# The first loads of v moved ahead of two pairs' q and k, and the first two pairs' splits shared out anew: a fused attention and MoE kernel

## The chip, the core and the metric

The kernel runs on one core of one Trainium2 chip. The metric is the device time of one execution in microseconds (us): the median of three runs. A core has TensorE (PE in the rows; PEld is its weight load), VectorE (DVE), ScalarE (ACT), GpSimd (POOL) and SyncE (SP). SP computes nothing here; it issues almost every transfer, one after the other, in the order in which the program was written. Each engine works off its own queue in order and waits on semaphores for the others.

## The reference

Causal attention over 2 batches x 12 heads, 448 positions, 64 channels a head, then two dense layers that the code calls MoE:

```python
scores = (q @ k.T) / 8;  scores = where(above the diagonal, -1e9, scores)
attn   = exp(scores - max);  attn = attn / (sum + 1e-9);  a = attn @ v       # per head
x = a laid out as 896 x 768
h = max(x@w1, x@w2, x@w3) @ w_out                # w1..w3: 768 x 768, w_out: 768 x 768
g = s * relu(h @ w_in)**2 + b                    # w_in: 768 x 2048
out = g @ w_out2                                 # 896 x 768
```

All inputs are float32. The kernel keeps float32 accuracy by writing each operand as a rounded part and a remainder, hi + lo, and by forming hi·hi + lo·hi + hi·lo on TensorE.

## The kernel before

The 24 heads are worked off as 12 pairs; one pair fills 128 partitions (two heads x 64 channels). `attention` runs 14 steps, `step(s)` for s = 0 to 13. In step s, three pairs are in flight: `new` = s (scores, minima, exponentials), `old` = s - 1 (transposes of the exponentials, row sums) and `out` = s - 2 (the product with v, `pv`). The MoE layers follow, with TensorE fed by decoded weight tiles.

A pair's data comes in as the tile `R`, 128 x (q, k) x 448, by `load(p)` (L268): 448 KB, one transfer, except pair 0, which comes in two. The pool behind `R` has four buffers, so pairs 0 to 3 are loaded ahead of step 0 and `load(4)` stands at the end of step 0. From `R` the tile `HL` is made: q hi, q lo, k hi, k lo. For pair 0 that is `split_now` (L330 to L340), called for columns 0 to 255 and for 256 to 447; for pair 1 it is `split_hi_early` on GpSimd and `split_lo_early` on VectorE. For pairs from 2 on, `scaled` (L296) multiplies q in `R` by -1/8 on GpSimd, `split_hi` (L309) rounds q and k on VectorE, and `split_lo` (L92) takes the remainders on GpSimd. `both_tails` copies the last 64 columns into the tile `bd` (L296). The order on GpSimd is the program's: `bd` of pair 0; hi of pair 1; `bd` of pair 1; `scaled(2)`, `scaled(3)`; a memset in `v` (L596); lo of pair 2; `bd` of pair 2; a memset in `v` (L606); lo of pair 3; `bd` of pair 3; `scaled(4)`.

The scores are written to PSUM (tiles A, B and C). `minima` (L396) takes row minima on VectorE, `exps` (L408) writes `p` on ScalarE, `transposes` (L435) turns `p` on TensorE, `pt_copy` (L441) brings it back. `pv` (L451, L455, L460) multiplies by v into the tile `o`, of which there is one buffer.

The row sums take a round trip through DRAM. `spread` copies them to `rows` (L487, VectorE) and SP writes them out as `rcd` (L488, L489). `broadcast` reads them back, spread over 64 partitions, as `rb` (L497, two transfers). `pv_out` (L506, VectorE) multiplies `o` by `rb` into `xf`. The next `pv` can't write `o` before that. `rcd` and `rb` of pair s - 1 are issued in step s; `xf` of pair s - 3 is computed in step s.

v comes in as four groups of pairs (`V_GROUPS`: first pair, number of pairs), each as seven pieces, and for a group of more than one pair as seven pieces for each head. Their elements are 256 bytes long. `V_LOADS` says how many pieces each step issues, before and behind its `rb`; 42 pieces in all. `FETCH` names the steps that fetch a weight tile `wraw` (L129, 768 KB).

The transfers share eight completion semaphores (DMAHW0 to DMAHW7 in the order below), given out in turn: a transfer waits on SP until the one eight before it has landed, and everything behind it on SP waits with it.

Of the kernel before, what the change touches and what calls it, by code (L numbers as in the profile page):

```python
# [14 lines left out]
ALU = mybir.AluOpType  # L15
# [9 lines left out]
NQ = 3  # L25
# [10 lines left out]
    7: ("low2",), 8: ("clamp2",), 9: ("shift2",), 10: ("hi1", "sign2"), 11: ("high3",),  # L36
    12: ("hi2", "low3"),
}
V_GROUPS = ((0, 1), (1, 1), (2, 4), (6, 6))
V_LOADS = ((7, 7), (2, 5), (3, 4), (3, 0), (3, 0), (3, 0), (3, 0), (2, 0))  # L40
FILL = {12: (3, 5), 13: (0, 4)}
WARM = 10
BUSY = (7,)
# [7 lines left out]
def kernel(  # L51
# [14 lines left out]
    nc = tc.nc  # L66
    n_pairs = qk.shape[0]
    S = qk.shape[3]
# [10 lines left out]
    scale = 1.0 / float(D) ** 0.5  # L79
# [11 lines left out]
    def sub_lo(eng, lo, full, hi):  # L91
        eng.tensor_tensor(out=lo, in0=full, in1=hi.bitcast(F32), op=ALU.subtract)  # L92
# [139 lines left out]
    def attention():  # L232
        with ExitStack() as c2:
# [10 lines left out]
            vs = [  # L244
                fixed.tile([128, n, 2, NQ + 1, D], F32, name=f"v{a}") for a, n in V_GROUPS
            ]
# [18 lines left out]
            def load(p, cuts=((0, S),)):  # L265
                pair[p]["R"] = R = ld.tile([128, 2, S], F32, tag="R", name="R")
                for a, b in cuts:
                    nc.sync.dma_start(out=R[:, :, a:b], in_=qk[p, :, :, a:b])  # L268
# [4 lines left out]
            def v_loads(g):  # L273
                (first, n), V = V_GROUPS[g], vs[g]
                for a, b in pieces:
# [7 lines left out]

            v_list = [e for g in range(len(V_GROUPS)) for e in v_loads(g)]

            def load_v(n):
                for _ in range(min(n, len(v_list))):
                    to, of = v_list.pop(0)
                    nc.sync.dma_start(out=to, in_=of)  # L289

            def v_of(p):
                g = max(g for g, (a, _) in enumerate(V_GROUPS) if a <= p)
                return vs[g][:, p - V_GROUPS[g][0]]

# [27 lines left out]
            def split_lo_early(p):  # L322
                HL, R = pair[p]["HL"], pair[p]["R"]
                nc.vector.scalar_tensor_tensor(
                    out=HL[:, 1], in0=R[:, 0], scalar=-scale, in1=HL[:, 0].bitcast(F32),
                    op0=ALU.mult, op1=ALU.subtract,
                )
                sub_lo(nc.vector, HL[:, 3], R[:, 1], HL[:, 2])

            def split_now(p, a, b, eng):  # L330
                HL, R = pair[p]["HL"], pair[p]["R"]
                q, k = (R[:, n, a:b] for n in range(2))
                qh, ql, kh, kl = (HL[:, n, a:b] for n in range(4))
                nc.vector.tensor_scalar(out=qh, in0=q, scalar1=-scale, scalar2=None, op0=ALU.mult)
                nc.scalar.copy(out=kh, in_=k)
                nc.vector.scalar_tensor_tensor(
                    out=ql, in0=q, scalar=-scale, in1=qh.bitcast(F32),
                    op0=ALU.mult, op1=ALU.subtract,
                )
                sub_lo(eng, kl, k, kh)  # L340

            def both_tails(p):
                HL = pair[p]["HL"].bitcast(F32)
# [27 lines left out]
            def at(p, i):  # L371
                a, b = ((2 * TQ, 3 * TQ), (0, 2 * TQ), (0, 3 * TQ))[i]
                return pair[p]["A" if i == 2 else "B"][:, :, a:b]
# [19 lines left out]
            def minima(p, i):  # L393
                e = pair[p]
                src, cols = (at(p, i), slice(2 * i, 2 * i + 2)) if i < NQ else (e["C"][:, 0:S], slice(2 * NQ, 2 * NQ + 1))
                nc.vector.tensor_reduce(  # L396
                    out=e["mx"][:, cols], in_=src, axis=mybir.AxisListType.X, op=ALU.min
                )
# [115 lines left out]

            CUT = 2 * TQ
            load(0, ((0, CUT), (CUT, S)))
            for p in range(1, 4):
                load(p)
            keep_busy(WARM)
            make_identity(nc, ident)  # L520
# [3 lines left out]
                out=tri.rearrange("p (a n) -> p a n", a=2), in_=tri.rearrange("p (a n) -> p a n", a=2), pattern=[[0, 2], [-1, TQ]], base=0, channel_multiplier=1,  # L524
# [8 lines left out]
            for P in ps:  # L533
                nc.gpsimd.memset(P[:, L0 + S:PW], 0.0)
            new_hl(0)
            split_now(0, 0, CUT, nc.vector)
            split_now(0, CUT, S, nc.gpsimd)
            both_tails(0)
            split_hi_early(1)
            first = early_products()  # L540
# [10 lines left out]
            def step(s):  # L551
                new, old, out, nxt = (
                    p if 0 <= p < n_pairs else None for p in (s, s - 1, s - 2, s + 2)
                )
                loads = V_LOADS[s] if s < len(V_LOADS) else (0, 0)
                if new is not None:
# [29 lines left out]
                    mask_c(new)  # L586
                    scores_c(new)
                if new == 0:
                    for i in (0, 1, 2, NQ):
                        minima(new, i)  # L590
                    split_lo_early(1)
                    both_tails(1)
                    for n in (2, 3):
                        scaled(n)
                    for V in vs[:2]:
                        nc.gpsimd.memset(V[D:128, :, :, NQ, :], 0.0)  # L596
                elif new is not None:
                    minima(new, 2)
# [43 lines left out]
                if old is not None:  # L642
# [2 lines left out]
                        spread(old)  # L645
                    transposes(old, 2)
                    transposes(old, 3)
                if new == 0:
                    load_v(loads[0])
                if s + 4 < n_pairs:  # L650
                    load(s + 4)
                if old is not None:
# [174 lines left out]
    with tc.manual_schedule():  # L827
        attention()
        moe()
# [50 lines left out]
```

## Time and profile before

| | us |
|---|---|
| median of 3 runs | 502.41 (501.32 to 503.15) |
| profiled execution, its own time | 502.06 |
| its span, first instruction to last | 500.3 |
| PE busy / DVE / ACT / POOL | 493.3 / 340.5 / 282.9 / 71.4 |
| PE's granted clock, mean | 0.999 of full speed |

The span is what the trace covers; the execution's own time is 1.76 us more, around it. Times in rows count from the span's start. A row of the timeline gives start, duration, engine, line, operation, tiles written and read, shapes, how many instructions are merged (x2), and in brackets how long the engine had been idle just before and what ended that. SPq is SP issuing a transfer: its duration is the issue, not the transfer. A busy PE is a modelled figure, so small gaps in it are rough.

### The profile page before, as it was taken

The page shows a single profiled execution, that of the slowest core. Times are in us where ns is not written, and L with a number is a line of the kernel's source. Part 1 is how long each engine was busy: PE and PEld are TensorE (multiplying, and loading weights), DVE is VectorE, ACT ScalarE, POOL GpSimd, SP SyncE. Part 2 cuts the span into 40 slices and gives each one's busy share as a digit, 9 for nine tenths or more (in the row PEclk, how much of TensorE's full clock was granted, in tenths as well). Part 3 has the DMA queues.
Part 4 walks back from the last instruction along what each step waited for, and adds up shares of the span by engine and source line. Part 5 has one row for each costly group of instructions (what it writes and reads, how often), then busy time and mean ns, then how long its engine had stood idle before and what let it go on. Part 6 is the DMA issues. An engine that isn't in the chain of part 4 may idle for free.

```text
span 500.3 us, 7557 instructions
## 1 busy us (share of the span) xinstructions
PE 493.3 (99%) x2909; PEld 452.7 (90%) x2909; DVE 340.5 (68%) x512; ACT 282.9 (57%) x527; POOL 71.4 (14%) x103
## 2 busy tenths in 40 slices
PE   8999999999999999999999999999999999999997
PEld 4877888899999999999999999999999999999996
DVE  5778896665857667587677888888888644484401
ACT  5988977444445254444546878888786432253101
POOL 6988992300000000000000000000000000000000
PEclk9999999999999999999999999999999999999999
DMA  5777534223324231333223323332333323261003
GB/s 170 225 215 226 151 102 117 103 91 127 126 75 148 94 126 64 126 128 126 101 89 126 127 73 118 126 104 85 127 126 109 119 89 128 88 220 56 1 0 111
DMA packets 26212, 58.34 MB, mean 117 GB/s; under 512 B 13548, under 2 KB 17600, under 8 KB 26176
## 3 DMA queue, kind: packets, MB, share of 16 engines
q1 hardware_dynamic: 26032, 57.76, 35.2%
q8 instruction: 23, 0.38, 0.3%
q14 instruction: 13, 0.11, 0.1%
q10 hardware_dynamic: 144, 0.10, 0.1%
HBM read 55.05 MB, written 2.80 MB: 116 GB/s over the span
## 4 chain that ended last, share of the span: by engine, by line
PE 91%; DMA 2%; DVE 2%; SPq 2%; ACT 1%; POOL 1%; issue 0%; DVEq 0%; ACTq 0%
PE m L698 58%; PE m L807 23%; PE t L435 3%; PE o L451 2%; ACT p L408 1%; PE o L455 1%; SPq L289 1%; PE A L380 1%; PE C L388 1%; PE B L380 1%; DMA rcd<-rows 1%; DMA rb<-rcd 1%; DMA R<-in_qk_dram 1%; POOL HL L92 0%; PE o L460 0%
## 5 line engine op out<-in xcount | busy, mean ns | idle before, releaser
L698 PE MATMUL m<-x,whi 128*128 128x448 f32 x816 | 232.0, 366 | 0.0
L698 PEld LDWEIGHTS m<-x,whi 128*128 128x128 f32 x816 | 153.1, 188 | 12.3 <-ACT p L408 0.2
L698 PE MATMUL m<-x,wlo 128*128 128x448 f32 x408 | 149.0, 365 | 0.0
L807 PE MATMUL m<-whi,g 128*128 128x384 f32 x448 | 114.0, 334 | 0.0
L184 ACT CAST whi<-wa 128x768 fp32r<-128x768 f32 x56 | 46.7, 833 | 67.0 <-PE m L807 43.8
L698 PEld LDWEIGHTS m<-x,wlo 128*128 128x128 f32 x408 | 76.6, 188 | 6.0
L807 PEld LDWEIGHTS m<-whi,g 128*128 128x128 f32 x448 | 81.0, 188 | 0.0
L144 ACT ACTIVATE wa<-wraw 128x768 f32<-128x768 f32 x56 | 50.6, 904 | 52.3 <-DVE wlo L92 52.3
L92 DVE TENSOR_TENSOR wlo<-wa,whi 128x768 fp32r<-128x768 f32 x56 | 53.3, 953 | 38.4 <-ACT whi L184 38.4
L807 PE MATMUL m<-wlo,g 128*128 128x384 f32 x224 | 74.8, 334 | 0.0
L179 DVE CUSTOM_DVE_ANT_0 wa<-wa,wr 128x1536 uint16<-128x1536 uint16 x56 | 53.6, 957 | 1.9
L172 DVE SCALAR_TENSOR_TENSOR wa<-wraw,wa 128x768 int32<-128x768 int32 x56 | 53.7, 959 | 0.0
L147 ACT ACTIVATE wr<-wraw 128x768 int32<-128x768 uint32 x56 | 50.6, 904 | 0.0
L807 PEld LDWEIGHTS m<-wlo,g 128*128 128x128 f32 x224 | 42.0, 188 | 0.0
L705 DVE TENSOR_TENSOR t<-t,m 128x448 f32<-128x448 f32 x24 | 14.9, 621 | 38.7 <-PE m L698 38.7
L698 PE MATMUL m<-h,whi 128*128 128x448 f32 x144 | 40.9, 365 | 0.0
L166 DVE TENSOR_SCALAR wa<-wa 128x768 int32<-128x768 int32 x56 | 32.2, 575 | 1.8
L92 POOL TENSOR_TENSOR HL<-R,HL 128x448 fp32r<-128x448 f32 (+1 forms) x21 | 29.9, 1443 | 3.2 <-DVE HL L309 2.1
L792 ACT ACTIVATE r<-m 128x448 f32<-128x448 f32 x32 | 17.4, 544 | 22.2 <-PE m L698 22.2
L698 PEld LDWEIGHTS m<-h,whi 128*128 128x128 f32 x144 | 27.1, 188 | 2.1
L158 DVE TENSOR_SCALAR wa<-wa 128x768 f32<-128x768 f32 x52 | 28.7, 552 | 0.0
L781 DVE SCALAR_TENSOR_TENSOR r<-m,r 128x448 f32<-128x448 f32 x32 | 20.0, 625 | 12.3 <-ACT r L792 12.3
(85 smaller groups left out, 551.2 us busy)
## 6 DMA issues: line engine op xcount, KB each, us to landing
wraw<-in_w_dram SPq DMA_DIRECT2D x56, 768.0 KB
R<-in_qk_dram SPq DMA_DIRECT2D x11, 448.0 KB
rb<-rcd SPq DMA_DIRECT2D x24, 112.0 KB
out_dram<-o SPq DMA_DIRECT2D x13, 192.0 KB
v<-in_v_dram SPq DMA_DIRECT2D x4, 96.0 KB
v<-in_v_dram SPq DMA_DIRECT2D x2, 168.0 KB
v<-in_v_dram SPq DMA_DIRECT2D x6, 48.0 KB
v<-in_v_dram SPq DMA_DIRECT2D x2, 144.0 KB
```

Source lines behind the costliest of these rows:

```text
L92: eng.tensor_tensor(out=lo, in0=full, in1=hi.bitcast(F32), op=ALU.subtract)
L144: nc.scalar.activation(out=e["f"], in_=e["high"].bitcast(F32), func=ACTF.Abs)
L147: nc.scalar.activation(out=e["r"], in_=e["low"].bitcast(U32), func=ACTF.Copy, scale=2.0 ** -29)
L158: nc.vector.tensor_scalar(out=e["f"], in0=e["f"], scalar1=UNDER, scalar2=OVER, op0=ALU.max, op1=ALU.min)
L166: nc.vector.tensor_scalar(out=a, in0=a, scalar1=3, scalar2=0x3FFFFFF8, op0=ALU.logical_shift_left, op1=ALU.bitwise_and,)
L172: nc.vector.scalar_tensor_tensor(out=e["a"], in0=e["high"], scalar=-0x40000000, in1=e["a"], op0=ALU.bitwise_and, op1=ALU.bitwise_or,)
L179: nc.vector.tensor_tensor(out=e["a"], in0=e["a"], in1=e["r"], op=ALU.add)
L184: nc.scalar.copy(out=e["hi"], in_=e["f"])
L698: nc.tensor.matmul(p, wt[w][:, ws], cols(act[i], a, b), start=(i == 0 and n == 0), stop=(i == len(act) - 1 and n == 2),)
L781: nc.vector.scalar_tensor_tensor(out=r, in0=p, scalar=0.0, in1=r, op0=ALU.max, op1=ALU.mult)
L792: after(0, lambda: nc.scalar.activation(out=r, in_=p, func=ACTF.Relu))
L807: nc.tensor.matmul(acc[t][:, 0:EH], gt[f][:, a, ts], w[:, ws], start=(f == 0 and n == 0), stop=(f == KG - 1 and n == 2),)
```

## The change

Three things change. On SP, the first seven pieces of v go ahead of the loads of pairs 2 and 3; the groups of v become pairs 0, 1, 2 to 4 and 5 to 11 (they were 0, 1, 2 to 5 and 6 to 11); and the pieces are given to other steps: 11 behind the weight tile in step 0, 4 and 6 in step 1, none in step 2, then 4, 4, 3 and 3 in steps 3 to 6, all ahead of `rb`. In `split_now`, columns 256 to 447 of q hi go from VectorE to ScalarE, and k lo of the same columns from GpSimd to VectorE. On VectorE, the minimum of pair 0's tile C goes from ahead of pair 1's q lo to behind it.

```diff
-V_GROUPS = ((0, 1), (1, 1), (2, 4), (6, 6))
-V_LOADS = ((7, 7), (2, 5), (3, 4), (3, 0), (3, 0), (3, 0), (3, 0), (2, 0))
+V_GROUPS = ((0, 1), (1, 1), (2, 3), (5, 7))
+V_LOADS = ((0, 11), (4, 6), (0, 0), (4, 0), (4, 0), (3, 0), (3, 0))
...
                     op0=ALU.mult, op1=ALU.subtract,
                 )
+                minima(0, NQ)
                 sub_lo(nc.vector, HL[:, 3], R[:, 1], HL[:, 2])
 
-            def split_now(p, a, b, eng):
+            def split_now(p, a, b):
...
-                nc.vector.tensor_scalar(out=qh, in0=q, scalar1=-scale, scalar2=None, op0=ALU.mult)
                 nc.scalar.copy(out=kh, in_=k)
+                if a:
+                    nc.scalar.mul(out=qh, in_=q, mul=-scale)
+                    sub_lo(nc.vector, kl, k, kh)
+                else:
+                    nc.vector.tensor_scalar(
+                        out=qh, in0=q, scalar1=-scale, scalar2=None, op0=ALU.mult
+                    )
                 nc.vector.scalar_tensor_tensor(
                     out=ql, in0=q, scalar=-scale, in1=qh.bitcast(F32),
                     op0=ALU.mult, op1=ALU.subtract,
                 )
-                sub_lo(eng, kl, k, kh)
+                if not a:
+                    sub_lo(nc.vector, kl, k, kh)
...
             load(0, ((0, CUT), (CUT, S)))
-            for p in range(1, 4):
+            load(1)
+            load_v(7)
+            for p in range(2, 4):
                 load(p)
...
-                    for i in (0, 1, 2, NQ):
+                    for i in range(NQ):
                         minima(new, i)
...
-                if new == 0:
-                    load_v(loads[0])
                 if s + 4 < n_pairs:
                     load(s + 4)
```

SP at the start of the program, before; R_135 is pair 0, R_138, R_140 and R_142 are pairs 1 to 3, R_251 is pair 4:

```order
L268 DMA R_138<-in_qk_dram 128x896
L268 DMA R_140<-in_qk_dram 128x896
L268 DMA R_142<-in_qk_dram 128x896
L289 DMA v0_112<-in_v_dram 112x2x64
L289 DMA v0_112<-in_v_dram 16x2x64
L289 DMA v0_112<-in_v_dram 96x2x64
L289 DMA v0_112<-in_v_dram 32x2x64 [waits DMAHW0_49]
L289 DMA v0_112<-in_v_dram 80x2x64 [waits DMAHW1_49]
L289 DMA v0_112<-in_v_dram 48x2x64 [waits DMAHW2_49]
L289 DMA v0_112<-in_v_dram 64x2x64 [waits DMAHW3_49]
L268 DMA R_251<-in_qk_dram 128x896 [waits DMAHW4_49,DVE_49,Pool_49]
L129 DMA wraw_253<-in_w_dram 128x768 [waits DMAHW5_49]
```

The same place now; R_138, R_147 and R_149 are pairs 1 to 3, R_251 is pair 4:

```order
L268 DMA R_138<-in_qk_dram 128x896
L289 DMA v0_112<-in_v_dram 112x2x64
L289 DMA v0_112<-in_v_dram 16x2x64
L289 DMA v0_112<-in_v_dram 96x2x64
L289 DMA v0_112<-in_v_dram 32x2x64
L289 DMA v0_112<-in_v_dram 80x2x64
L289 DMA v0_112<-in_v_dram 48x2x64 [waits DMAHW0_49]
L289 DMA v0_112<-in_v_dram 64x2x64 [waits DMAHW1_49]
L268 DMA R_147<-in_qk_dram 128x896 [waits DMAHW2_49]
L268 DMA R_149<-in_qk_dram 128x896 [waits DMAHW3_49]
L268 DMA R_251<-in_qk_dram 128x896 [waits DMAHW4_49,DVE_49]
L129 DMA wraw_253<-in_w_dram 128x768 [waits DMAHW5_49]
```

The loads of pairs 2 and 3 moved behind seven pieces of v, and the first of them now waits for DMAHW2, the landing of pair 1's load.

SP from the end of step 1 to pair 1's `rb` in step 2, before (v2_114 is the third group of v):

```order
L289 DMA v2_114<-in_v_dram 96x4x64 [waits DMAHW7_49]
L289 DMA v2_114<-in_v_dram 32x4x64 [waits DMAHW0_49]
L129 DMA wraw_355<-in_w_dram 128x768 [waits DMAHW1_49]
L488 DMA rcd_447<-rows_446 7x128 [waits DMAHW2_49,DVE_49]
L489 DMA rcd_447<-rows_446 1x64 [waits DMAHW3_49]
L268 DMA R_462<-in_qk_dram 128x896 [waits DMAHW4_49,Pool_49]
L289 DMA v2_114<-in_v_dram 32x4x64 [waits DMAHW5_49]
L289 DMA v2_114<-in_v_dram 80x4x64 [waits DMAHW6_49]
L289 DMA v2_114<-in_v_dram 80x4x64 [waits DMAHW7_49]
L497 DMA rb_448<-rcd_447 64x448 [waits DMAHW2_49,DMAHW0_49]
L497 DMA rb_448<-rcd_447 64x448 [waits DMAHW3_49,DMAHW1_49]
```

The same place now:

```order
L289 DMA v2_114<-in_v_dram 48x3x64 [waits DMAHW5_49]
L289 DMA v2_114<-in_v_dram 64x3x64 [waits DMAHW6_49]
L289 DMA v2_114<-in_v_dram 64x3x64 [waits DMAHW7_49]
L129 DMA wraw_362<-in_w_dram 128x768 [waits DMAHW0_49]
L496 DMA rcd_454<-rows_453 7x128 [waits DMAHW1_49,DVE_49]
L497 DMA rcd_454<-rows_453 1x64 [waits DMAHW2_49]
L268 DMA R_469<-in_qk_dram 128x896 [waits DMAHW3_49,Pool_49]
L505 DMA rb_455<-rcd_454 64x448 [waits DMAHW4_49,DMAHW1_49]
L505 DMA rb_455<-rcd_454 64x448 [waits DMAHW5_49,DMAHW2_49]
```

The third group's pieces are all ahead of the weight tile now, and none is left between `rcd` and `rb`, nor behind `rb` (four were).

VectorE at the start, before (HL_173 is pair 0's, HL_184 pair 1's; the columns of a row's shape tell the two parts of pair 0 apart):

```order
L334 TENSOR_SCALAR HL_173<-R_135 128x192 [waits DMAHW1_49]
L336 SCALAR_TENSOR_TENSOR HL_173<-R_135,HL_173 128x192 [waits DVE_49]
L396 TENSOR_REDUCE mx_187<-B_189 128x2 [waits PE_49]
L396 TENSOR_REDUCE mx_187<-B_189 128x2
L396 TENSOR_REDUCE mx_187<-A_204 128x2 [waits PE_49]
L396 TENSOR_REDUCE mx_187<-C_213 128x1 [waits PE_49]
L324 SCALAR_TENSOR_TENSOR HL_184<-R_138,HL_184 128x448 [waits DMAHW2_49,Pool_49]
L92 TENSOR_TENSOR HL_184<-R_138,HL_184 128x448 [waits Pool_49]
```

The same place now (HL_180 is pair 0's, HL_191 pair 1's):

```order
L92 TENSOR_TENSOR HL_180<-R_135,HL_180 128x192 [waits DMAHW1_49,Activation_49]
L343 SCALAR_TENSOR_TENSOR HL_180<-R_135,HL_180 128x192 [waits Activation_49]
L404 TENSOR_REDUCE mx_194<-B_196 128x2 [waits PE_49]
L404 TENSOR_REDUCE mx_194<-B_196 128x2
L404 TENSOR_REDUCE mx_194<-A_211 128x2 [waits PE_49]
L324 SCALAR_TENSOR_TENSOR HL_191<-R_138,HL_191 128x448 [waits DMAHW2_49,Pool_49]
L404 TENSOR_REDUCE mx_194<-C_220 128x1 [waits PE_49]
L92 TENSOR_TENSOR HL_191<-R_138,HL_191 128x448 [waits Pool_49]
```

A subtraction stands where a multiplication stood, and the minimum of C moved behind an instruction that waits for GpSimd and for pair 1's load.

## Rows read from the trace of the kernel before

**Rows 1.** Windows: stretch, its us, busy us of each engine, clock, DMA share, GB/s.

```profile
30.00:35.00 5.00, 3.92 (x39) 3.00 (x37) 3.36 (x7) 3.75 (x14) 3.46 (x6) 1.00 0.41 102
35.00:40.00 5.00, 4.43 (x43) 3.81 (x42) 3.47 (x7) 4.71 (x14) 4.25 (x5) 1.00 0.95 244
```

**Rows 2.** Timeline of PE, steps 0 to 5.

```profile
4.90 1.03 PE L380 MATMUL B<-HL 64*128 64x128 f32 x12
...
10.95 1.09 PE L435 MATMUL t<-ident,p 128*128 128x128 f32 x8
...
21.88 0.27 PE L350 MATMUL A<-tri,identb 128*128 128x128 bf16 x2
...
28.26 0.27 PE L350 MATMUL A<-tri,identb 128*128 128x128 bf16 x2
...
32.89 0.59 PE L451 MATMUL o<-PT,v 128*64 128x448 f32 x1 [1.08 <-DVE xf L506]
...
40.21 0.59 PE L451 MATMUL o<-PT,v 128*64 128x448 f32 x1 [0.78 <-DVE xf L506]
```

**Rows 3.** Chain that ended last: start, us, what.

```profile
0.73 3.31 DMA R<-in_qk_dram
...
93.11 287.17 PE m L698 x1416
```

**Rows 4.** Timeline of DVE.

```profile
5.06 0.65 DVE L334 TENSOR_SCALAR HL<-R 128x192 fp32r<-128x192 f32 x1
...
8.92 0.97 DVE L324 SCALAR_TENSOR_TENSOR HL<-R,HL 128x448 fp32r<-128x448 f32 x1 [0.39 <-POOL HL L296]
...
21.01 0.63 DVE L309 CAST HL<-R 128x896 fp32r<-128x896 f32 x1 [1.95 <-POOL R L296]
21.55 0.27 DVE L487 COPY rows<-A 7x128 f32<-7x128 f32 x1
...
32.21 0.62 DVE L506 TENSOR_TENSOR xf<-o,rb 128x448 f32<-128x448 f32 x1 [1.64 <-DMA rb<-rcd]
...
39.53 0.62 DVE L506 TENSOR_TENSOR xf<-o,rb 128x448 f32<-128x448 f32 x1 [1.33 <-DMA rb<-rcd]
...
93.28 0.62 DVE L506 TENSOR_TENSOR xf<-o,rb 128x448 f32<-128x448 f32 x1 [2.96 <-DMA rb<-rcd]
```

**Rows 5.** Timeline of POOL.

```profile
8.32 1.09 POOL L296 TENSOR_SCALAR HL<-R 128x448 fp32r<-128x448 f32 x2 [1.38 <-DMA R<-in_qk_dram]
...
11.03 1.09 POOL L296 TENSOR_SCALAR R<-R 128x448 f32<-128x448 f32 x2
...
20.41 0.56 POOL L296 TENSOR_SCALAR R<-R 128x448 f32<-128x448 f32 x1
```

**Rows 6.** Timeline of SP.

```profile
3.70 6.42 SPq L289 DMA_DIRECT2D v<-in_v_dram  x7
...
8.20 0.57 SPq L289 DMA_DIRECT2D v<-in_v_dram  x1
...
11.00 0.35 SPq L268 DMA_DIRECT2D R<-in_qk_dram  x1
...
11.86 4.47 SPq L289 DMA_DIRECT2D v<-in_v_dram  x7
...
19.93 2.56 SPq L289 DMA_DIRECT2D v<-in_v_dram  x5
...
23.07 0.29 SPq L488 DMA_DIRECT2D rcd<-rows  x1
...
35.02 1.12 SPq L497 DMA_DIRECT2D rb<-rcd  x2
...
87.47 0.27 SPq L488 DMA_DIRECT2D rcd<-rows  x1
...
89.73 1.09 SPq L497 DMA_DIRECT2D rb<-rcd  x2
```

**Rows 7.** Timeline of ACT.

```profile
9.85 0.66 ACT L408 ACTIVATE p<-C,mx 128x448 f32<-128x448 f32 x1
```

More of the change, by code (lines that the diff above doesn't have):

```diff
@@ L535, in attention @@
             new_hl(0)
-            split_now(0, 0, CUT, nc.vector)
-            split_now(0, CUT, S, nc.gpsimd)
+            split_now(0, 0, CUT)
+            split_now(0, CUT, S)
             both_tails(0)
```

## The prediction

> **What bounds the kernel now.** I read four views in this order: busy time by stretch, the timelines of TensorE, VectorE, GpSimd and SP over the first 45 us, and the chain that ended last.
>
> The chain ends in one long run of TensorE work: from 93.11 on, 287 us of the first layers' products follow one another [rows 3]. Whatever the attention stage gains or loses before that shifts this run as a whole, so a microsecond there is a microsecond of the span. The change touches only the attention stage.
>
> In that stage TensorE is short of work in two places. From 30 to 35 it is busy 3.92 of 5 us, from 35 to 40 it is 4.43 of 5 [rows 1]. The timeline says why: the product with v stood still 1.08 us at 32.89 (step 4) and 0.78 us at 40.21 (step 5), both times for `xf` on VectorE [rows 2], and VectorE had waited 1.64 and 1.33 us for `rb` [rows 4]. So VectorE may be about 0.55 late there at no cost to TensorE. `rb` is a round trip through DRAM whose transfers SP issues among the pieces of v. Steps 3 to 4 with no such wait take 28.26 - 21.88 = 6.38 us [rows 2].
>
> A third bound stands earlier. At 21.01 VectorE had waited 1.95 us for GpSimd's `scaled(4)`, which ran from 20.41 [rows 4, 5]; the copy of the row sums stands behind that cast and ends at 21.82, and the first mask of step 3, which writes the bank that the copy read, starts at 21.88 [rows 2, 4]. GpSimd thus sets when step 3 begins, with about 0.06 us to spare. It runs almost without a gap from 11.03, `scaled(2)` and `scaled(3)`, to that `scaled(4)` [rows 5].
>
> **The change, part by part.** *Pairs 2 and 3 loaded later (a loss).* Before, SP got past the semaphores of the loads of pairs 1 and 3 at 8.20 and at 11.00, which is 1.40 us for each of two transfers [rows 6]. Now seven pieces of v come first. Five loads took SP from 0.73 to 3.70, 0.59 each [rows 3, 6], so three end at 2.5; seven pieces of a one-pair group took 4.47 [rows 6], so SP is through at 7.0. The load of pair 2 then waits for pair 1's landing, 8.20 if that stays, 7.0 or less if it comes sooner. An issue on an idle queue took 3.3 us to its first user [rows 3]: pair 2 lands at 10.3 to 11.5, pair 3 1.4 later, at 11.7 to 12.9. `scaled(3)` takes half of 1.09 [rows 5] and ends at about 12.3 to 13.5, where it ended at 12.12. GpSimd's chain to `scaled(4)` is therefore 0.2 to 1.4 us later, and step 3 with it. I take 1.1, near the upper end, since 8.20 is the one landing that a row shows.
>
> Here the rows are weighed against a rule. Before, the three loads were passed 1.40 apart, one after the other, though all were issued by 3.70 [rows 6]. The Trainium skill, DMA: Bandwidth & Descriptors, section Queues, rings and completion order, says that each DMA engine takes its descriptors in the order of its ring. By that rule the loads behind pair 1 never slowed it, it lands no sooner now, and the loss is the upper end, 1.4, which makes the sum below +0.6. If the loads shared the bandwidth instead, pair 1 would land by 7.0, and the sum would be -0.6. The spacing of the rows agrees with the rule.
>
> *SP reaches pair 1's row sums later, but finds fewer pieces behind them.* The first piece of v's third group is the eighth transfer behind step 0's weight tile, so SP can't issue it before that tile has landed. With pair 3 at 12.6, pair 4 lands 1.4 later and the tile (768 KB against 448 KB at 1.40) 2.4 after that, at 16.4. From there SP issues all 14 pieces of the third group (5 took 2.56 [rows 6], so 7.2), and about 2.5 for two `rcd`, a load, two `rb` and a weight tile: it comes to pair 1's `rcd` at about 26.1, where it was 23.07 [rows 6]. Bounds by the same sum: 25.2 and 26.4. From `rcd` to `xf` it took 32.21 - 23.07 = 9.14 us [rows 4, 6], with three pieces of v in between and a weight tile ahead; on the quiet queue at the end of attention it took 93.28 - 87.47 = 5.81 [rows 4, 6]. The three pieces are gone, the tile is still right ahead of `rcd` (2.4 us of transfer, issued half a microsecond earlier), a load follows: I take 7.2, the quiet trip and 1.4 of the tile. So `xf` can run at 33.3. VectorE would be ready for it at 32.21 - 1.64 + 1.1 = 31.7. The wait is 1.6, as it was, and step 4 keeps its 1.08 of idle TensorE. Between the bounds it goes from no wait (25.2 + 5.8 = 31.0: a gain of 1.08) to 3.5 us (26.4 + 9.1 against 32.0: idle 3.0, a loss of 1.9). If pair 1 lands sooner, VectorE and SP come sooner alike, so this term hardly hangs on the first.
>
> *No pieces of v in step 2 (a gain).* Pair 2's `rb` was issued at 35.02 and used at 39.53, 4.5 later [rows 4, 6]. SP is now free for pair 2's `rcd` when pair 1's `rb` is out: `rcd` to `rb` took 89.73 - 87.47 = 2.26 on the quiet queue [rows 6], with 1.4 for the tile ahead 3.7, and 1.1 for the two issues, so 26.1 + 4.8 = 31; a `rcd`, a load and four pieces take 3.2, so `rb` goes at 34.2. The four pieces are 448 KB against 360 KB in three, by the rate of the loads 0.3 us more, so it lands at 39.0. VectorE, 1.1 later than before, wants it at 39.53 - 1.33 + 1.1 = 39.3. The wait of step 5 is gone: -0.78. Bounds: 0 and -0.8.
>
> *Steps 3 to 6 carry more of v ahead of `rb`* (7 pairs a piece instead of 6). By the same sum pair 3's `rb` has more than 1 us to spare; pair 5's last pieces are issued one step ahead of their use. I count nothing; without that cover it is the transfer of the last pieces, at most 0.5.
>
> *The splits of pair 0.* VectorE's 0.65 for 192 columns [rows 4] goes to ScalarE, GpSimd's subtraction to VectorE: by the 0.43 and 0.36 that its neighbours need, VectorE ends between 0.4 sooner and 0.2 later. The first minimum needs the scores of B, which end at 5.93 [rows 2] and do not read these columns. So 0; if ScalarE came later than that, 0.2 at most.
>
> *The minimum of C behind pair 1's q lo.* That instruction started at 8.92, after GpSimd, and ended at 9.89 [rows 4]. The minimum of C comes after it, about 0.6 for 448 columns as the exponential needed 0.66, so the exponential of C starts at 10.5 instead of 9.85 [rows 7] and ends at 11.2; the transposes that read it started at 10.95 [rows 2]. That is up to 0.3 us in step 1, and if pair 1 lands at 7.0 it is nothing. It lies beside the 1.1 on GpSimd's chain, which alone sets step 3. I add 0.
>
> **The sum.** +1.1, 0 and -0.78 give +0.3. The profiled execution took 502.06 (span 500.3 and 1.76 around it): 502.4 after. It lies 0.35 below the median of 502.41: the median after is 502.7. With the bounds of the first term alone the likeliest case reaches from 501.8 to 503.2.
>
> **The rivals.** *Both waits go and the late loads cost little.* Pair 1 lands by 7.0, pair 3 costs 0.2, and pair 1's round trip is the quiet one: 25.2 + 5.8 = 31.0 against 30.8 needed and 0.55 to spare. Then 0.2 - 1.08 - 0.78 = -1.7: 500.7. For it: the pieces of v behind `rb` and between `rcd` and `rb` are gone. Against it: the weight tile stays directly ahead of `rcd`, and the spacing of the loads.
>
> *Slower: the weight tile, landing late, holds SP, and pair 1's row sums come out too late.* Place: SP in step 1, at the first piece of the third group. Landing as before takes 9.1 us: 26.4 + 9.1 = 35.5, which makes the idle time of step 4 3.0 instead of 1.08. With 1.4 for GpSimd and the gain of step 5: 1.4 + 1.9 - 0.78 = +2.5, 504.9. It decides against the kernel by more than 0.3% once `xf` of step 4 comes 1.2 us later than I have it. For it: the SP queue is 3 us late by every sum. Against it: three pieces fewer in the trip.
>
> *The change only moves the waits.* Pair 2's `rb` is late as well since the pieces of seven pairs lie ahead of it; step 5 keeps half of its wait. Then +1.1 - 0.4 = +0.7: 503.1.
>
> **How the numbers follow.** The likeliest case has 0.45, the fast rival 0.23, the slow one 0.14, the one that only moves waits 0.18. What a measurement of this kernel can tell from no change is about 0.3%, 1.5 us: below 500.9 or above 503.9. Faster: most of the fast rival and a little of the likeliest, 0.22. Slower: the slow rival and the upper part of the one that moves waits, 0.20. Within: 0.58. The range runs from 500.6 to 504.4: it takes in the fast rival and leaves out the far end of the slow one.
>
> **What would show it.** `scaled(3)` ending near 13.2 and step 3's first mask near 23.0 would show the first step right; an end by 12.3 would show it wrong. SP's `rcd` of pair 1 near 26 and `xf` of step 4 still waiting about 1.6 for `rb` would show the second; no wait there makes the forecast wrong to the fast side. No wait at step 5's `xf` shows the third. The product with v in steps 2 and 7 waiting on a transfer of v would be a cost that I left out.

## The result, and the profile after

The changed kernel takes 506.28 us (median of 15 runs, 504.50 to 508.30) against 502.60 for 15 runs of the kernel before beside them: ratio 1.0072, interval 1.0056 to 1.0088. It is slower by 3.7 us, where I had forecast no change, and the median lies outside my range. Two things make it up. The profiled execution shows 2.4 us of new waits (span 502.7 against 500.3; its own time, 504.50, is the shortest of the 15). And the runs fall into two groups by TensorE's mean granted clock: six at 0.999 or more take 504.5 to 505.4, nine at 0.995 to 0.997 take 506.2 to 508.3. The profiled one is of the first group, so the second thing isn't in it; an experiment below shows it. Of the 15 runs of before none lies above 504.9. Three runs of kernels further down, of 540.57, 697.18 and 1255.03 us, count as slow and are in none of the figures.

Where the 2.4 us come from is read at the first mask of each step on TensorE (a step begins there), before and after:

| first mask of step | before | after | later by |
|---|---|---|---|
| 1 | 10.03 | 9.93 | -0.10 |
| 3 | 21.88 | 22.45 | 0.57 |
| 4 | 28.26 | 29.16 | 0.90 |
| 5 | 35.86 | 37.95 | 2.09 |
| 6 | 43.10 | 44.34 | 1.24 |
| 7 | 49.50 | 50.73 | 1.23 |
| 8 | 55.87 | 58.04 | 2.17 |
| 11 | 75.31 | 77.76 | 2.45 |

Step 1 begins at nearly the same time in these two profiles. That is not always so: over the 19 profiles of this document it begins between 9.87 and 11.07. Where two profiles differ there, times are counted from step 1.

Timeline of TensorE in the changed kernel: start, duration, line, operation, and in brackets the idle time ahead and its releaser (answers to [rows 2]).

```profile
22.45 0.27 PE L358 MATMUL A<-tri,identb 128*128 128x128 bf16 x2 [0.32 <-DVE rows L495]
29.16 0.27 PE L358 MATMUL A<-tri,identb 128*128 128x128 bf16 x2
34.99 0.59 PE L459 MATMUL o<-PT,v 128*64 128x448 f32 x1 [2.27 <-DVE xf L514]
37.95 0.28 PE L358 MATMUL A<-tri,identb 128*128 128x128 bf16 x2
44.34 0.28 PE L358 MATMUL A<-tri,identb 128*128 128x128 bf16 x2
50.73 0.28 PE L358 MATMUL A<-tri,identb 128*128 128x128 bf16 x2
56.79 0.33 PE L468 MATMUL o<-PT,v 128*64 128x64 f32 x2 [0.40 <-DMA v<-in_v_dram]
58.04 0.28 PE L358 MATMUL A<-tri,identb 128*128 128x128 bf16 x2
```

Three places lose and one gains. Step 3 begins behind GpSimd. Step 4's product with v stands still 2.27 us instead of 1.08. In step 5 nothing waits any more (the 0.78 is gone). In step 7 the product waits for pieces of v, which it did not before.

VectorE (answers to [rows 4]) and SP (answers to [rows 6]) show the second of them.

```profile
21.58 0.63 DVE L309 CAST HL<-R 128x896 fp32r<-128x896 f32 x1 [2.33 <-POOL R L296]
25.39 0.62 DVE L514 TENSOR_TENSOR xf<-o,rb 128x448 f32<-128x448 f32 x1 [0.56 <-DMA rb<-rcd]
34.31 0.62 DVE L514 TENSOR_TENSOR xf<-o,rb 128x448 f32<-128x448 f32 x1 [2.82 <-DMA rb<-rcd]
40.19 0.57 DVE L514 TENSOR_TENSOR xf<-o,rb 128x448 f32<-128x448 f32 x1
```

```profile
7.27 1.55 SPq L268 DMA_DIRECT2D R<-in_qk_dram  x3
...
9.34 9.02 SPq L289 DMA_DIRECT2D v<-in_v_dram  x11
18.46 0.32 SPq L496 DMA_DIRECT2D rcd<-rows  x1
...
19.55 1.92 SPq L289 DMA_DIRECT2D v<-in_v_dram  x4
21.56 1.15 SPq L505 DMA_DIRECT2D rb<-rcd  x2
22.76 3.43 SPq L289 DMA_DIRECT2D v<-in_v_dram  x6
26.23 0.60 SPq L129 DMA_DIRECT2D wraw<-in_w_dram  x1
26.93 0.29 SPq L496 DMA_DIRECT2D rcd<-rows  x1
...
30.57 1.35 SPq L505 DMA_DIRECT2D rb<-rcd  x2
```

The row sums of pair 1 wait in SP's list behind six pieces of v and a weight tile: `rcd` goes out at 26.93 instead of 23.07, `rb` at 30.57, and VectorE has been ready for it for 2.82 us at 34.31. ScalarE too waits 2.07 us for that weight tile (at 32.35), in the shadow of the same wait.

GpSimd in the changed kernel (answers to [rows 5]) shows the first loss:

```profile
7.17 1.10 POOL L296 TENSOR_SCALAR HL<-R 128x448 fp32r<-128x448 f32 x2 [0.71 <-DMA R<-in_qk_dram]
...
11.40 0.57 POOL L296 TENSOR_SCALAR R<-R 128x448 f32<-128x448 f32 x1 [1.44 <-DMA R<-in_qk_dram]
12.48 0.58 POOL L296 TENSOR_SCALAR R<-R 128x448 f32<-128x448 f32 x1 [0.51 <-DMA R<-in_qk_dram]
...
20.98 0.57 POOL L296 TENSOR_SCALAR R<-R 128x448 f32<-128x448 f32 x1
```

`scaled(2)` and `scaled(3)` each wait for their load, the second ends at 13.06 instead of 12.12, and `scaled(4)` comes 0.57 later: just what step 3's mask is later.

### The profile page after: what moved, and what is told of

Its sections match the earlier page's. It is cut to its first block, busy times and chain, and to the rows that moved or that the text cites. A ratio compares the mean times of both kernels' runs of the same rounds, so it can differ in the third digit from the quotient of the medians.

```text
span 502.7 us, 7555 instructions
## 1 busy us (share of the span) xinstructions
PE 493.9 (98%) x2909; PEld 452.7 (90%) x2909; DVE 341.5 (68%) x512; ACT 283.4 (56%) x528; POOL 70.0 (14%) x102
## 4 chain that ended last, share of the span: by engine, by line
PE 88%; DMA 4%; SPq 2%; ACT 2%; DVE 1%; POOL 1%; issue 1%; DVEq 0%; POOLq 0%
PE m L706 58%; PE m L815 23%; PE t L443 2%; PE o L459 1%; SPq L289 1%; DMA rb<-rcd 1%; ACT p L416 1%; DMA R<-in_qk_dram 1%; PE o L463 1%; DMA v<-in_v_dram 1%; DMA rcd<-rows 1%; PE A L388 1%; POOL HL L92 1%; PE B L388 1%; SPq L268 1%
## 5 line engine op out<-in xcount | busy, mean ns | idle before, releaser
L92 POOL TENSOR_TENSOR HL<-R,HL 128x448 fp32r<-128x448 f32 x20 | 28.4, 1440 | 3.5 <-DVE HL L309 3.3
```

## The experiments

Ratios are to runs of the kernel before on the same chip, taken beside those of the changed one.

**The two halves apart.** The kernel before with only the new groups and order of the queue, and the kernel before with only the new splits and the moved minimum.

> The kernel before with the new order of SP's queue and the new groups of v alone; splits and the minimum of C as before. Theory Q (the queue makes the loss: pairs 2 and 3 land later, pair 1's rcd goes out 4 us later behind the weight tile, the last pieces of v come too late in step 7): as slow as the changed kernel, ratio 1.005 to 1.009 (505 to 507 us), xf of step 4 waiting about 2.8 us for rb, step 7's pv waiting on v. Rival S (the new splits and the minimum behind pair 1's q lo make it): 1.000 +- 0.002.

> The kernel before with the new splits and the moved minimum alone; SP's queue as before. Theory Q: 1.000 +- 0.002, step 3's first mask within 0.4 us of 21.88, the waits of 1.64 and 1.33 us for rb still there. Pair 1 lands near 8.2, so VectorE should stand idle ahead of pair 1's q lo and C's exponential should start near 10.5. Rival S: 1.005 or more.

Measured: the queue alone 506.47, 1.0065 (1.0046 to 1.0085); the splits alone 502.52, 0.9991 (0.9979 to 1.0003). The queue is all of it. Its profiled execution is of the second group, and a window over step 4's product with v shows what that is: stretch, its length, busy us and instructions of PE, PEld, DVE, ACT and POOL, granted clock, DMA share, GB/s. First the queue alone, then the changed kernel.

```profile
36.00:39.30 3.30, 3.30 (x23) 2.18 (x20) 1.93 (x4) 1.72 (x8) 2.59 (x4) 0.50 1.11 225
```

```profile
36.00:39.30 3.30, 3.30 (x42) 2.89 (x40) 3.11 (x6) 3.17 (x13) 2.68 (x2) 1.00 0.99 183
```

At a granted clock of 0.50, which is 1.2 instead of 2.4 GHz, TensorE is busy throughout and issues 23 products where the other issues 42. The fall lasted from 35.88 to 39.29. TensorE had stood still just before:

```profile
35.63 0.81 PE L451 MATMUL o<-PT,v 128*64 128x448 f32 x1 [2.66 <-DVE xf L506]
40.21 0.28 PE L350 MATMUL A<-tri,identb 128*128 128x128 bf16 x2
```

Step 4 took 10.79 us (29.42 to 40.21) where the changed kernel's profile has 8.79; 0.39 of the 2.00 is the longer idle time, the other 1.61 go with the half clock. Two theories followed. Q: SP's place in its own list times pair 1's `rb`. C: TensorE's long idle time there brings the half clock.

In the kernel with the splits alone the wait of step 4 was 0.48 and that of step 5 2.26, though its queue is that of before (1.64 and 1.33 there [rows 4]): these waits differ by an execution as much as by a small edit, so single waits of one profile are read with that much play.

**The last pieces of v sooner; the weight tile sooner.** Changed kernel, with 4, 5, 5 pieces in steps 3 to 5, and changed kernel with step 1's weight tile ahead of the six pieces:

```diff
-V_LOADS = ((0, 11), (4, 6), (0, 0), (4, 0), (4, 0), (3, 0), (3, 0))
+V_LOADS = ((0, 11), (4, 6), (0, 0), (4, 0), (5, 0), (5, 0))
```

```diff
+                if s == 1:
+                    fetch_w()
                 load_v(loads[1])
-                if s in FETCH:
+                if s in FETCH[1:]:
```

> The changed kernel with the last group's pieces given to steps 3, 4 and 5 (4, 5 and 5) instead of steps 3 to 6 (4, 4, 3, 3). Theory Q: the wait of pv on v in step 7 goes, and with it 0.9 us: 0.998 of the changed kernel, about 1.005 to 1.006 of the one before; the wait of step 4 stays at 2 to 3 us. If the two pieces more in step 5 hold its rb, a new wait at step 6's xf takes part of it back. Rival (the idle TensorE in step 4 lowers its clock in many executions, and the rest of the loss is that): the time goes down by 0.9 but executions with a granted clock of 0.995 to 0.997 remain, and are 1.5 to 3 us longer than those at 0.999 to 1.000.

> The changed kernel with step 1's weight tile issued ahead of the six pieces of v behind pair 0's rb, instead of behind them. Theory Q with the tile as what holds pair 1's row sums: rcd no longer lands behind 768 KB, rcd to rb falls from 3.6 to about 2.5 us, step 4's wait from 2.8 to about 1.7, its idle TensorE from 2.3 to 1.1: 0.9976 of the changed kernel, 1.005 of the one before. Rival (SP's lateness alone does it, 26.9 instead of 23.1): no change, 1.007.

Measured: 505.71, 1.0061 (1.0042 to 1.0081), and 505.86, 1.0045 (1.0026 to 1.0065). Neither is a cure. With the pieces sooner, SP's list up to pair 1's `rb` is that of the changed kernel, but the profiled run (508.70 us; seven of nine runs had a clock of 0.996 or 0.997) has 4.31 us of idle time in step 4, where I expected 2 to 3:

```profile
37.00 1.01 PE L459 MATMUL o<-PT,v 128*64 128x448 f32 x1 [4.31 <-DVE xf L514]
```

The chains of work that ended last (start, us, what) show why: pair 1's `rcd`, at the same place of the list, took 3.63 us in the changed kernel's profile and 5.58 in this one, and SP can't issue `rb` before it has landed.

```profile
26.93 3.63 DMA rcd<-rows
```

```profile
27.35 5.58 DMA rcd<-rows
```

Step 7's wait for v is gone in that kernel, and `rb`, which now has five pieces ahead of it, is late there:

```profile
58.90 0.62 DVE L514 TENSOR_TENSOR xf<-o,rb 128x448 f32<-128x448 f32 x1 [2.25 <-DMA rb<-rcd]
```

With the tile sooner the second transfer of `rcd` was held up, since a transfer takes the completion semaphore of the one eight earlier, and that was the tile's:

```profile
27.43 0.44 SPq L496 DMA_DIRECT2D rcd<-rows  x1
29.98 0.24 SPq L497 DMA_DIRECT2D rcd<-rows  x1
```

Step 4's idle time was 2.06 there, not the 1.1 that I expected, and the clock fell in three of eight runs.

**Longer idle time in the kernel before, by the queue.** The kernel before with the tile directly behind pair 0's `rb`, and the kernel before with all seven pieces of step 2 ahead of `rb` (`(3, 4)` to `(7, 0)`).

> The kernel before with step 1's weight tile issued directly behind pair 0's rb, ahead of five pieces of v, instead of behind them. Theory Q: pair 1's rcd (4.0 us from issue to landing) no longer lands behind 768 KB, rb of pair 1 goes out 1 to 1.5 us sooner, step 4's idle of 1.1 us goes and step 5's (0.8) at least shrinks: 0.9965 +- 0.0015 of the kernel before. Rival (SP's place in its queue alone, not what lies on the DMA queues, times rcd to rb): no change, 1.000 +- 0.001.

> The kernel before with step 2's seven pieces of v all ahead of pair 1's rb (three ahead and four behind before). SP stood 1.4 us waiting for rcd's landing there, and the four pieces behind rb then held pair 2's rcd until 32.1. Theory Q: rb of pair 1 goes out about 0.7 us later and lands behind four more pieces, step 4's idle grows from 1.1 to 2 us or more, while pair 2's rcd goes out 3 us sooner and step 5's idle of 0.8 goes. In sum 1.000 to 1.003. Rival (pieces ahead of rb are free as long as SP waits anyway): 0.998 to 0.9985.

Measured: 504.96, 1.0033 (1.0020 to 1.0046), the wrong way for my expectation, and 504.62, 1.0030 (1.0017 to 1.0042). In the first, SP's next load waited for the tile's semaphore until 26.96, so `rb` went out at 29.93 instead of 27.12; in the second at 29.30. TensorE stood still 2.67 and 2.35 us in step 4, and the clock was 0.996 or 0.997 in three of six and four of eight runs. So a loss of the same kind, 0.3% of the changed kernel's 0.7%, can be made in the kernel before by SP's list alone. The second of them also shows a limit: the seven pieces between `rcd` and `rb` kept SP until 29.25, past the 27.12 at which `rb` had gone out.

**The loads of pairs 2 and 3 ahead of v again, in the changed kernel.**

> The changed kernel with the loads of pairs 1 to 3 ahead of pair 0's v again; all else as changed. Theory Q: scaled(3) ends near 12.1 again and step 3's mask goes back by 0.6 us, but pair 1's rcd still goes out about 3 us later than before, behind the tile and all of the third group, and step 7's wait on v stays. So 0.6 us of the loss comes back, 1.005 to 1.006. Rival (the late loads of pairs 2 and 3 are what makes everything behind them late): the waits of step 4 fall back to 1.1 us, 1.001 to 1.003.

Measured: 506.66, 1.0067 (1.0047 to 1.0088): nothing is won that this measurement can tell. In its profile step 3 comes 11.72 us behind step 1 (12.52 in the changed kernel, 11.85 before), so what the late loads cost is gone again; but step 1 began 1.06 later, `rcd` of pair 1 went out at 27.12 (26.93 in the changed kernel), and TensorE stood still 2.75 us in step 4. The late loads, which my first term was about, are a small part of the loss, and not what makes the wait of step 4.

**TensorE kept busy in step 4.** Changed kernel with eight products of constants ahead of step 4's product with v (`BUSY = (7, 0, 0, 0, 8)`).

> The changed kernel with eight dummy 512-column products on TensorE (1.7 to 2 us) ahead of step 4's pv, where TensorE stood idle 2.3 us and more. Nothing else changes, so the waits stay. Theory C (in most executions of the changed kernel TensorE's granted clock falls to half for 3.4 us in step 5, right after that idle stretch, and that is 1.7 to 2 us on top of the waits): the granted clock of all executions is 0.999 to 1.000 and the median falls to that of the undipped executions, 504.5 to 505.4, ratio 1.004 to 1.005. Rival (the dip has nothing to do with the idle stretch): executions at 0.995 to 0.997 remain and the time stays at 1.0065 to 1.007, or is later by what the products add.

Measured: 507.51, 1.0086 (1.0065 to 1.0107). They had to wait for ScalarE's copy, which stood behind the late weight tile, and began only at the end of the idle time:

```profile
35.83 1.91 PE L521 MATMUL warm<-const-bfloat16-1.0 128*128 128x512 bf16 x7 [2.77 <-ACT PT L449]
```

The clock was 0.999 or more in four of six runs, but they added 1.9 us themselves. That tells nothing between C and its rival, so I made the idle time in the kernel before, without touching the queue: four extra minima on VectorE, to a spare tile, ahead of step 4's `xf`, first reading A, then (clean) reading the split q in SBUF; each with and without products of constants on TensorE.

```diff
+                if s == 4:
+                    for _ in range(4):
+                        nc.vector.tensor_reduce(
+                            out=spare, in_=pair[new]["HL"].bitcast(F32)[:, 0:2, 0:384],
+                            axis=mybir.AxisListType.X, op=ALU.min
+                        )
                 if 0 <= s - 3 < n_pairs - 2:
```

> The kernel before with four extra minima of A in step 4, written to a spare tile, right in front of that step's product with rb on VectorE: nothing else changes, and the queue is that of before. Four such minima take about 3.5 us, 1.6 of them lie in the wait that stood there, so xf comes 1.8 us later and TensorE's idle time in front of pv grows from 1.08 to about 2.9. Theory C (a long idle of TensorE in step 4 makes the granted clock fall to half for some 3 us, which costs about 2 us more): some or most executions show a clock of .995 to .997, step 4 is about 4 us longer than before in those, step 5's wait (0.78) goes, median 504.5 to 506, ratio 1.004 to 1.007. Rival N (the clock falls for another reason, such as the queue's own traffic, and idle time costs only itself): clock .998 or more, +1.8 - 0.78, ratio 1.001 to 1.003.

> The same kernel as the one with four extra minima, and TensorE given eight products of constants, 512 columns each (about 1.7 us), to do in front of step 4's pv, in the time in which it would wait for that late xf. ScalarE is on time here, so the bank they write should be free at about 32.2. The wait on VectorE is the same, so what idle time itself costs is the same. Theory C: the clock stays at .998 or more, and this kernel is 1.5 to 2 us faster than the other one although it does more, ratio 1.001 to 1.003. Rival N: the same time as the other kernel or up to 0.3 us later.

> The kernel before with four extra minima on VectorE in front of step 4's xf, as in the kernel with the late xf, but they read the split q in SBUF and not A, so ScalarE's exponentials need not wait for them. xf comes at about 34.0 instead of 32.2, TensorE's idle time grows from 1.08 to about 2.9. Theory C (idle time of TensorE brings the half clock): clock .995 to .997 in most runs, ratio 1.004 to 1.007, of it 1.1 us the wait (1.8 less 0.78 of step 5) and the rest the clock. Rival N: .998 or more, ratio 1.001 to 1.003.

> The same kernel, and TensorE given ten products of constants (512 columns each, about 2.1 us together) in front of step 4's pv. ScalarE is on time, so they start at about 32.3 and end at about 34.4, when xf ends: the wait on VectorE is the same and TensorE stands still for only 0.5 of it. Theory C: clock .998 or more in nearly all runs, and 1.5 to 2 us faster than the same kernel without the products: ratio 1.001 to 1.003. Rival N: no faster than without them, 1.004 to 1.008 if the clock falls all the same.

Measured: with A, 505.90 (1.0060, 1.0043 to 1.0077), all six at 0.995 or 0.996; its profile shows 3.15 us of idle time. Filled, 509.56 (1.0133): ScalarE's exponentials had to wait for the minima that read the same bank (4.11 us), so the filling came 4.43 late, and the clock was half for 6.83 us. That one miscarried. The clean pair did not. Without filling 505.68, 1.0056 (1.0043 to 1.0069), five runs from 505.02 to 506.06, all at 0.995 or 0.996. With filling 1.0032 (1.0019 to 1.0045), five runs from 503.94 to 505.15, all at 0.998 or more. Their TensorE rows, without and with:

```profile
35.22 1.01 PE L452 MATMUL o<-PT,v 128*64 128x448 f32 x1 [3.14 <-DVE xf L507]
...
38.63 0.28 PE L481 MATMUL A<-ident,su 128*7 128x128 f32 x1
```

```profile
33.28 2.35 PE L514 MATMUL warm<-const-bfloat16-1.0 128*128 128x512 bf16 x10 [0.46 <-ACT PT L442]
35.96 0.59 PE L452 MATMUL o<-PT,v 128*64 128x448 f32 x1 [0.33 <-DVE xf L507]
...
37.94 0.28 PE L481 MATMUL A<-ident,su 128*7 128x128 f32 x1
```

and the windows over the wait and over the products behind it, without and with:

```profile
31.00:34.80 3.80, 1.08 (x10) 0.79 (x7) 3.70 (x5) 1.98 (x6) 1.05 (x3) 1.00 0.37 76
34.90:38.20 3.30, 2.98 (x16) 1.83 (x18) 2.61 (x5) 1.72 (x8) 2.25 (x3) 0.50 1.04 278
```

```profile
31.70:35.50 3.80, 3.34 (x20) 1.78 (x18) 3.70 (x5) 2.02 (x6) 0.99 (x3) 1.00 0.80 213
35.60:38.90 3.30, 2.97 (x32) 2.40 (x32) 3.25 (x7) 1.94 (x9) 2.20 (x3) 1.00 0.44 93
```

The same two kernels on VectorE, without and with:

```profile
30.77 3.86 DVE L610 TENSOR_REDUCE spare<-HL 128x2 f32<-128x768 f32 x4
34.55 0.61 DVE L507 TENSOR_TENSOR xf<-o,rb 128x448 f32<-128x448 f32 x1
```

```profile
31.51 3.86 DVE L610 TENSOR_REDUCE spare<-HL 128x2 f32<-128x768 f32 x4
35.29 0.61 DVE L507 TENSOR_TENSOR xf<-o,rb 128x448 f32<-128x448 f32 x1
```

`xf` starts 3.78 us behind the first extra minimum in both, so VectorE is as late in one as in the other. Where TensorE stood still 3.14 us, its clock is half and the product with v takes 3.41 us up to the row sums' transpose (35.22 to 38.63); where it had work to do, the clock stays and the product takes 1.98. Theory C is shown: with the wait on VectorE unchanged, it is TensorE's idle time that brings the fall. One fall costs 1.1 to 1.4 us, less than the 1.5 to 2 that I expected: 1.43 by these rows, 1.32 by the medians of five runs each (505.68 less 504.36) and 1.08 by their means. The Trainium skill, TensorE: Matmul & The Clock Gate, section Why this matters for your kernels, advises against long idle times of the array between bursts since its clock drops; this pair agrees (half clock after 3.14 us of idle time, full clock where only 0.46 and 0.33 were left).

**The changed kernel mended by its list alone.** Four pieces from ahead of the tile and pair 1's `rcd` to between its `rcd` and `rb`, where SP waits anyway; and the same with the last group's pieces out a step sooner, one each behind `rb`.

```diff
-V_LOADS = ((0, 11), (4, 6), (0, 0), (4, 0), (4, 0), (3, 0), (3, 0))
+V_LOADS = ((0, 11), (4, 2), (4, 0), (4, 0), (4, 0), (3, 0), (3, 0))
```

```diff
+V_LOADS = ((0, 11), (4, 2), (4, 0), (4, 1), (4, 1), (4, 0))
```

> The changed kernel with four pieces of v's third group moved from ahead of the weight tile and of pair 1's row sums (step 1) to between that pair's rcd and rb (step 2), where SP waits anyway. Theory QC (SP's place makes the idle time of step 4, and that brings the half clock): rcd of pair 1 goes out at about 24.7 instead of 26.93, rb at about 28.3 instead of 30.57, step 4's idle time falls from 2.27 to 0.5 to 1.5, the clock stays at .998 or more in most runs; the waits of steps 3 (0.57) and 7 (0.9) stay. Ratio 1.000 to 1.003. Rival W (the tile's own landing holds ScalarE and rb whatever the place): idle time above 2, clock falls, 1.005 to 1.007.

> As the kernel with the rows ahead of four pieces, and the last group's 14 pieces out by step 5 instead of 6, one each in steps 3 and 4 behind rb instead of more ahead of it. The wait for v in step 7 (0.9) goes and no new wait for rb comes: ratio 0.9985 to 1.001, 0.9 us faster than the other kernel of this call. Rival: the pieces behind rb push back the next rcd, step 6 or 7 waits for rb instead, and nothing is won.

Measured: 504.56, 1.0024 (1.0010 to 1.0037), all twelve runs at 0.999 or more; and 503.55, 1.0020 (1.0000 to 1.0040). In the first kernel `rcd` of pair 1 went out at 25.30 instead of 26.93, `rb` at 29.78 instead of 30.57, and `xf` ran at 34.29 instead of 34.31:

```profile
34.97 0.59 PE L459 MATMUL o<-PT,v 128*64 128x448 f32 x1 [1.89 <-DVE xf L514]
37.93 0.27 PE L358 MATMUL A<-tri,identb 128*128 128x128 bf16 x2
```

Only 0.38 of the idle time is gone (1.89 left, where I expected 0.5 to 1.5), since the transfers took longer: 4.48 from `rcd` to `rb` instead of 3.64, and 4.51 from there to `xf` instead of 3.74. So SP's place is a part of that wait, and not all of it. The ratio went from 1.0072 to 1.0024 all the same: no run has a fall of the clock any more. The waits that stay (steps 3, 4 and 7) hold it where the changed kernel's first group is. In the second kernel no wait for v is left in step 7 and the median is 1.0 us lower, as expected; but two of its twelve runs show 0.997, among them the profiled one, with 2.40 us of idle time in step 4, and by the ratios, 1.0024 and 1.0020, the two kernels are not told apart.

**A kernel ahead of both?** The kernel before with four pieces of v moved from behind pair 1's `rb` to between pair 2's `rcd` and `rb`; that and the tile fetched in step 3; and the first with the new splits.

```diff
-V_LOADS = ((7, 7), (2, 5), (3, 4), (3, 0), (3, 0), (3, 0), (3, 0), (2, 0))
+V_LOADS = ((7, 7), (2, 5), (3, 0), (4, 3), (3, 0), (3, 0), (3, 0), (2, 0))
```

> The kernel before with four pieces of v moved from behind pair 1's rb (step 2) to between pair 2's rcd and rb (step 3), and three from there to behind that rb. Theory Q (SP's place in its own list times rb): rcd of pair 2 goes out at about 28.5 instead of 32.13, its rb at about 32.3 instead of 35.02, so step 5's wait of 0.78 goes: ratio 0.998 to 0.999. Step 4's idle time of 1.08 stays, as the weight tile is still ahead of pair 1's rcd. Rival V: the third group of v lands after 32.9, and pv of step 4 waits for it: 1.000 to 1.002.

> As the kernel with the four pieces moved, and the second weight tile fetched in step 3, behind pair 2's rb, instead of step 1, ahead of pair 1's rcd; its first two operations on ScalarE go to steps 4 and 8. Theory Q: rcd of pair 1 goes out 0.4 us sooner and has no 768 KB ahead of it, so its rb is out at about 25.6 instead of 27.12 and xf of step 4 finds it there: the waits of 1.08 and of 0.78 both go, ratio 0.996 to 0.998. Rival V: the third group of v, due at 31.8 then, comes late by 0.5 to 1, ratio 0.998 to 1.000. ScalarE's extra operation in step 8 should cost nothing, else up to 0.5 us.

> The kernel before with the four pieces of v between pair 2's rcd and rb (0.9983 by itself) and the new splits of pair 0 with the minimum of C behind pair 1's q lo (0.9991 by itself). If they add up: 0.996 to 0.998. If the splits are worth nothing: 0.998 to 0.999.

Measured: 502.16, 0.9983 (0.9969 to 0.9997); 506.58, 1.0075; 502.89, 1.0003 (0.9989 to 1.0016). In the first, step 5's wait is gone, as expected, and the product of step 4 waits 0.33 for v in exchange. In the second the waits of steps 4 and 5 both went, as Q expects, but the moved tile, out at 35.00, reached ScalarE only at 41.55:

```profile
41.55 0.90 ACT L144 ACTIVATE wa<-wraw 128x768 f32<-128x768 f32 x1 [5.10 <-DMA wraw<-in_w_dram]
```

TensorE then stood still 3.02 us at 43.62, and its clock was half from 44.96 to 51.79. The third, with the same list as the first, does not repeat its gain. The two intervals overlap, so the gain of 0.17% is neither confirmed nor refuted, and none of these is safely ahead of the kernel before.

## Why the prediction was wrong

*Pairs 2 and 3 later: right in mechanism, half the size.* I took 1.1; step 3 is 0.57 later. `scaled(3)` ended at 13.06, near the 13.2 I gave, which is partly luck: SP got to pair 2's load at 7.27 and not at 8.20, and the load took 4.1 us to its first user (11.40) instead of the 3.3 that I took. The memset behind took 0.34 instead of 0.72, so that 0.57 of the 0.94 was left. Pair 1 was used at 7.17, against 8.32 before [rows 5]. Over all profiles it was used at 6.88 to 7.31 where pieces of v follow it (seven profiles) and at 7.01 to 8.50 where two loads do (twelve): as a rule it lands sooner without them, against what I drew from ring order in the Trainium skill (DMA: Bandwidth & Descriptors, Queues, rings and completion order). A ring taken in order does not mean that a transfer behind costs the one ahead nothing. (With my own terms the likeliest case ends at 503.0, not at 503.2; nothing hangs on it.)

*Pair 1's row sums: this is the step that failed.* I had `rcd` at 26.1 (at most 26.4), the way to `xf` at 7.2, `xf` at 33.3, VectorE ready at 31.7, and so a wait of 1.6 as before, for a term of 0. Measured are 26.93, 7.38, 34.31 and 31.49: three errors of 0.8, 0.2 and 0.2, all to the same side, make the wait 2.82 and the idle time 2.27, and step 4 is 1.19 longer. SP came to the third group at 16.51, where I had it at 16.4; from there to `rcd` it took 10.42 instead of 9.7. The 14 pieces took 7.20 of it, as I had them; two `rcd`, a load, two `rb` and a tile took 2.79 instead of 2.5, and 0.43 are gaps between these groups, which I had not counted. That is the shortest of the 15 runs, in which SP's lateness is 0.8 of the 1.2. In the profile with 4.31 us of idle time, of a kernel with the same list up to there, the way from `rcd` to `xf` took 8.97 (27.35 to 36.32), close to the 9.1 of my slow rival, so its late landing came on top. Its condition, `xf` 1.2 later than I had it, was nearly met with 1.0 in the first and met with 3.0 in the second. I gave it 0.14.

*What the idle time brings besides itself: absent.* No term, rival or bound spoke of the granted clock, since the kernel before shows 0.999. The clean pair puts 1.1 to 1.4 on a fall, and nine of 15 runs had one. The group means differ by 2.3 (507.25 and 504.94), more than a fall costs: the runs with a fall presumably had longer waits too. In the changed kernel that was not seen, as one execution is profiled; the two profiles with a fall and the same list up to pair 1's `rb` have them, with 2.66 and 4.31 us of idle time against 2.27.

*Step 5's wait gone: right.* -0.85 (7.24 to 6.39 between the masks of steps 5 and 6) against -0.78.

*More v ahead of `rb`: wrong.* I counted 0, and named pair 5's last pieces, at most 0.5, as the cost without cover. The chain of the changed kernel has 4.14 us of `v` ending there; the step took 7.31 instead of 6.37, 0.94 more. My last paragraph had named a wait in step 7 as a cost that I would have left out. The last three pieces went out at 51.45 to 53.24, one step ahead of their use, and the product waited for them at 56.79; the twin that has them out two steps ahead has no such wait, and its median is 1.0 lower. One step is not always too late: in the kernel before, the last two pieces went out in step 7, at 56.59, and step 8 did not stand still for them; other profiles with that list show 0.25 us at most.

*Also left out:* pair 0's `xf` in step 3 now waits 0.56 for `rb`, and the cast behind it on VectorE took 1.52 instead of 0.97; with the two, step 4 begins another 0.33 late, 0.90 in all. Steps 8 to 10 lose 0.3 more; 0.26 of it is a wait of step 9's product for `xf` (at 68.24).

*Splits and minimum of C: right.* The splits alone are 0.9991; step 1's mask is no later.

## What to carry to other kernels

Where one engine issues all transfers in order, lay out its list in time, gaps between issues too, and ask of each short round trip what stands ahead of it; put bulk transfers between its two halves, where the engine waits anyway, and not ahead of the first, but no more than fit in that wait (in the changed kernel four did, in the kernel before seven did not). A wait on TensorE is not worth its length alone: one that has grown past what the kernel had so far may take the clock with it, and then the work behind it runs at half clock: 3.41 us instead of 1.98 for step 4's product with v. Read the granted clock of every run, not only of the profiled one.

## What was not expected of the hardware

TensorE's clock falls to half within an attention stage that is otherwise dense, after a single stop: with 3.14 and 3.15 us in the profiles, in all eleven runs of those two kernels; in kernels whose profiles show 2.06 to 2.77, in some of the runs and not in others (nine of 15 of the changed kernel, with 2.27); with 4.31, in seven of nine; with 1.89, in none of twelve; and in at most one of the 13 to 23 runs of the kernel before that were taken beside each group of experiments (1.08 and 0.78 in its profile). These are the idle times of one profiled run of each kernel, and they differ from run to run. Their length does not decide alone: the profile with 2.06 us has a fall and the one with 2.75 has none. What else decides is not shown here. A kernel that waits about that long has times in two groups, and its median depends on how many runs fall on each side.
